# Everything behind attention as one list of steps, ordered for each engine by the kernel itself, with GpSimd's passes moved to VectorE

## The chip, the cores and the metric

One core of a Trainium2 chip. The metric is the device time of one execution in microseconds, as the median of several runs. All inputs and outputs lie in HBM; attention, two gated layers and their projections run in one launch.

## The reference

```python
attn_out = attention(q, k, v, tau)        # q, k, v: (4, 8, 576, 64); scores under max - tau are masked
x = attn_out.transpose(0, 2, 1, 3).reshape(2304, 512)

def moe(x, w_gate, w_val, w_out):         # 512 -> 1536 -> 512
    g = x @ w_gate
    return (g / (1 + exp(-g)) * (x @ w_val)) @ w_out

def moe2(x, w1, w2, w3, w_out):           # 512 -> 1024 -> 1024 -> 512
    return (((x @ w1) * (x @ w2)) @ w3) @ w_out

return moe2(moe(x, ...), ...)
```

The weights come as 64-bit floats (their product with a numpy scalar is one), the rest as 32-bit floats.

## The kernel before

**Number format.** TensorE multiplies in a rounded 32-bit format. Every operand of a large product is held as a pair: a rounded high half and the low half that is left (`high`, `rest`), and each product is three passes (`PASSES`: high x high, high x low, low x high). So for every tile that enters TensorE one engine copies it (ScalarE, the high half) and one subtracts (VectorE or GpSimd, the low half). A 64-bit weight of 128x512 arrives as words and is put together on the way: two mask passes and a combining pass on VectorE (`bits`, `more`), two activations on ScalarE (`conv_power`, L252 and L253), a difference on GpSimd (`conv_less`, L258), a multiply on VectorE (`value`, L1519). A weight "unit" is one such tile; its 512 KB land in a ring of three buffers (`raw`, L227).

**Tiling.** The 2304 tokens are five blocks (512, 512, 256, 512, 512; numbers 0 to 4); blocks 0 and 1 and blocks 3 and 4 form two pairs, block 2 is alone. The hidden width is cut into tiles f of 128. One projection of one block by one f is 12 matmuls of 512 columns (256 for block 2).

**Stages behind attention.**
1. First projections (`plain`): f = 0 to 2 of the gated layer for each block, two projections each. Each block's x is read back from HBM in two halves that GpSimd adds (`x_add`, L1407); TensorE spreads the reciprocal row sums over the partitions (L1422), VectorE multiplies (L1427) and ScalarE and VectorE split (`x_scale`). Beside this `panels` makes sums and differences of x blocks.
2. Gated stage, f = 3 to 11 (`glu_seq`): each pair of blocks takes seven products instead of eight (`seven`, slots p1 to p7 of six matmuls, L1704), with sums of weight blocks and of x panels. Two such chains run slot by slot beside each other, with block 2's two plain projections between (`run`). ScalarE copies intermediate sums out of a chain's bank before the next product adds to that bank (`snap`, L1718); VectorE adds (L1731, L1747, L1762); GpSimd multiplies (L1754, L1764). The result goes to HBM (`h_dram`).
3. Output projection: for each block over f = 0 to 11 four banks collect 12 matmuls per f; h is read back and split (L1942, L1948). x of the second layer is taken out of the banks (`evacuate`) and panels are made again.
4. Bilinear stage, f = 0 to 7: as stage 2 without the activation.
5. The product w3 @ w_out of the second layer (w3 turned on TensorE, L1464), held as "whole" tiles that were converted earlier and parked in HBM (`v_dram`).
6. Last stage: 18 tiles of 128 tokens, 24 matmuls each, then the store.

**What sets the order.** Attention runs by a plan of its own (`Plan`, in a manually scheduled section). Behind it the code issues work in program order, slot by slot, and after each slot calls `feed`/`tick` and `do`, which bring forward one piece of weight conversion and one of the queued pieces (panels, copies). `take` and `give` hand out a common pool of 42 slots of 128x2x512; `spare` and `promised` keep some back. The framework then orders the instructions for each engine with its own model of time. All transfers are issued on SyncE's queue (SP). The same two-chain stages use the banks of PSUM: two double banks S and four single banks T.

Of the kernel before, what the change touches and what calls it, by code (L numbers as in the profile page):

```python
# [28 lines left out]
PLAIN = 3  # L29

# [14 lines left out]
class Plan:  # L45
# [20 lines left out]
    def order(self):  # L66
# [51 lines left out]
        return [step for _, _, step in sorted(done, key=lambda d: d[:2])]  # L118


@with_exitstack
def kernel(
# [1336 lines left out]
    w3v = {}  # L1459

    def w3_turn(i, g, val):
        bank = t_bank()
        for c in range(4):
            nc.tensor.transpose(bank[:, c * P:(c + 1) * P], val[:, c * P:(c + 1) * P], ident)  # L1464
        un = take()
        nc.scalar.copy(out=un[:, 0, :], in_=bank)
        nc.vector.tensor_tensor(
            out=un[:, 1, :], in0=bank, in1=f32(un[:, 0, :]), op=ALU.subtract
        )
        w3v[i, g] = un  # L1470


    units, u_raw = deque(), deque()
    spare, promised = [0], [0]

    def pair_of(srcs, keys, sums=False, want=3):

        shared = {}
        for i, (src, key) in enumerate(zip(srcs, keys)):
            units.append(  # L1480
                {"src": src, "key": key, "i": i, "pair": shared, "sums": sums, "want": want})

    def u_fetch():
        while units and len(u_raw) + len(conv_raw) < N_BIG and units[0].get("raw") is None:
            u = units.popleft()
            u["raw"] = conv_load(u["src"])
            u_raw.append(u)

    def split(un, src, engine):
        nc.scalar.copy(out=un[:, 0, :], in_=src)  # L1490
        engine.tensor_tensor(out=un[:, 1, :], in0=src, in1=f32(un[:, 0, :]), op=ALU.subtract)

    def stages(u):

        pair, key = u["pair"], u["key"]
        if u["i"] == 0:
            pair["stage"] = take(F32)
        m = pair["stage"][:, u["i"], :]
        mi = m.bitcast(I32)
        if wide == 2:  # L1500
            two = u["raw"].rearrange("p (n t) -> p n t", t=2)
            a, x = two[:, :, 0], two[:, :, 1]
            low = u["raw"].bitcast(U16).rearrange("p (n t) -> p n t", t=4)[:, :, 1]

        def bits():
            nc.vector.tensor_scalar(
                out=mi, in0=x, scalar1=(1 << 20) - 1, scalar2=None, op0=ALU.bitwise_and
            )
            nc.vector.tensor_scalar(
                out=x, in0=x, scalar1=-(1 << 20), scalar2=None, op0=ALU.bitwise_and  # L1510
            )

        def more():
            nc.vector.scalar_tensor_tensor(  # L1514
                out=m, in0=low, scalar=2.0 ** -16, in1=mi, op0=ALU.mult, op1=ALU.add
            )

        def value():
            nc.vector.scalar_tensor_tensor(  # L1519
                out=m, in0=m, scalar=2.0 ** 20, in1=f32(a), op0=ALU.add, op1=ALU.mult  # L1520
            )

        def plain_copy():
            nc.vector.tensor_copy(out=m, in_=u["raw"])

        if wide == 2:
            yield bits
            yield more
            yield lambda: conv_power((a, mi, x))
            yield lambda: conv_less((a, mi, x))  # L1530
            yield value
        else:
            yield plain_copy
        if u["want"] == 1:
            if u["i"]:
                yield lambda: nc.sync.dma_start(out=v_dram[key], in_=pair["stage"])
                give(pair.pop("stage"))
            return

        def high(src, name):  # L1540
            def go():
                u[name] = take()
                promised[0] -= 1
                nc.scalar.copy(out=u[name][:, 0, :], in_=src)  # L1544
            return go

        def rest(src, name, key, engine):
            def go():
                un = wu[key] = u[name]
                engine.tensor_tensor(  # L1550
                    out=un[:, 1, :], in0=src, in1=f32(un[:, 0, :]), op=ALU.subtract
                )
            return go

        yield high(m, "un")
        yield rest(m, "un", key, nc.gpsimd)
        if u["sums"] and u["i"]:
            g, v = (pair["stage"][:, i, :] for i in range(2))
            b11, b21, b12, b22 = g[:, 0:2 * P], g[:, 2 * P:], v[:, 0:2 * P], v[:, 2 * P:]

            def less(*args):
                def go():
                    for out, x, y in args:
                        nc.vector.tensor_tensor(out=out, in0=x, in1=y, op=ALU.subtract)
                return go

            yield less((b11, b12, b11), (b12, b22, b12))
            yield less((b22, b22, b11), (b21, b21, b22))
            yield high(g, "c")
            yield rest(g, "c", ("c", key[1]), nc.vector)  # L1570
            yield high(v, "d")
            yield rest(v, "d", ("d", key[1]), nc.vector)
# [372 lines left out]
    def h_low():  # L1945
# [5 lines left out]
        if i:  # L1951
            give(t)
# [278 lines left out]
```

## Time and profile before

| | |
|---|---|
| median of 3 runs | 1149.25 us (1149.05 to 1150.66) |
| the profiled execution's own time | 1149.66 us |
| its span, first to last instruction | 1147.9 us |
| TensorE shown busy | 1073.8 us, 94% |
| VectorE, ScalarE, GpSimd busy | 829.4, 625.1, 609.5 us |
| mean granted clock of TensorE | 0.977 of full |

A busy TensorE in this profile is not one at its peak: its matmuls overlap, and a matmul that starts every 0.23 us is shown as 0.39 long. Time that TensorE loses is found by counting matmuls per stage, not from its busy share. PE is TensorE's matmul, PEld its weight load, DVE VectorE, ACT ScalarE, POOL GpSimd, SPq SyncE's queue of transfers.

### The profile page before, as it was taken

How to read it: one execution, taken by the hardware profiler on the slowest of the kernel's cores; microseconds unless marked ns; L12 is line 12 of the kernel's file. 1: busy time of each engine (PE TensorE's matmuls, PEld its weight loads, DVE VectorE, ACT ScalarE, POOL GpSimd, SP SyncE). 2: the span in 40 equal slices, each digit the busy share in tenths (PEclk: the TensorE clock that was granted, in tenths of full speed). 3: DMA queues.
4: the chain of work that ended last, by engine and by line, in shares of the span. 5: the costliest groups of instructions: out<-in, count | busy, mean ns of one | idle time of the engine just before them, and what ended most of it. 6: DMA issues, size and time to landing. Idle time of an engine off the chain costs nothing. (4 is left out here: it accounts for less than half of the span.)

```text
span 1147.9 us, 17303 instructions
## 1 busy us (share of the span) xinstructions
PE 1073.8 (94%) x5838; PEld 922.4 (80%) x5838; DVE 829.4 (72%) x1432; ACT 625.1 (54%) x1284; POOL 609.5 (53%) x547
## 2 busy tenths in 40 slices
PE   7999999999987999899999798999999899999998
PEld 6989898999666787678788686888788788788887
DVE  7999999999769758888775877933989863444110
ACT  6898989899734355446465445533545433333100
POOL 5898989987546126445565765633554332213100
PEclk9999999999897999999999899999999999999999
DMA  6776776766572114434336755331144423733312
GB/s 170 176 204 173 186 183 168 181 152 167 153 224 94 61 68 160 130 127 163 115 136 207 249 161 186 103 87 42 62 157 159 156 83 134 263 108 102 110 50 52
DMA packets 127208, 162.39 MB, mean 141 GB/s; under 512 B 48688, under 2 KB 83312, under 8 KB 127120
## 3 DMA queue, kind: packets, MB, share of 16 engines
q1 hardware_dynamic: 126976, 161.29, 47.3%
q8 instruction: 46, 0.75, 0.3%
q14 instruction: 42, 0.34, 0.1%
q10 hardware_dynamic: 144, 0.00, 0.0%
HBM read 93.47 MB, written 44.19 MB: 120 GB/s over the span
## 5 line engine op out<-in xcount | busy, mean ns | idle before, releaser
L1438 PE MATMUL t_bank<-slot,slot 128*128 128x512 f32 (+1 forms) x1536 | 316.1, 358 | 0.7 <-ACT slot L1428 0.7
L1438 PEld LDWEIGHTS t_bank<-slot,slot 128*128 128x128 f32 x1536 | 265.4, 190 | 48.7 <-ACT slot L1428 1.1
L1704 PE MATMUL t_bank<-slot,slot 128*128 128x512 f32 x816 | 206.6, 396 | 11.9 <-ACT tmp L1718 11.8
L1704 PEld LDWEIGHTS t_bank<-slot,slot 128*128 128x128 f32 x816 | 152.9, 191 | 45.1 <-ACT tmp L1718 14.0
L1704 PE MATMUL s_bank<-slot,slot 128*128 128x512 f32 x612 | 160.6, 398 | 9.7 <-DVE tmp L1762 4.3
L258 POOL TENSOR_TENSOR raw<-raw 128x512 int32<-128x512 int32 x76 | 91.8, 1212 | 105.2 <-ACT raw L253 80.3
L1704 PEld LDWEIGHTS s_bank<-slot,slot 128*128 128x128 f32 x612 | 113.0, 190 | 35.9 <-DVE tmp L1762 4.9
L202 POOL TENSOR_TENSOR AT<-tmp,AT 128x512 fp32r<-128x512 f32 x102 | 132.2, 1306 | 3.4
L252 ACT ACTIVATE raw<-raw,ebias 128x512 int32<-128x512 int32 x76 | 58.4, 770 | 133.0 <-DVE slot L1514 89.9
L557 ACT ACTIVATE P<-P,stat 128x576 f32<-128x576 f32 x144 | 113.9, 795 | 7.4 <-DVE P L548 7.0
L548 DVE SCALAR_TENSOR_TENSOR P<-E,stat,s_bank 128x576 f32<-128x576 f32 x144 | 114.4, 808 | 1.5
L532 DVE TENSOR_SCALAR_CACHE_REDUCE E<-s_bank 128x576 f32<-128x576 f32 x144 | 107.2, 754 | 8.2 <-PE s_bank L500 7.0
L500 PE MATMUL s_bank<-R,L 128*128 128x288 f32 x512 | 94.8, 308 | 12.6 <-DVE P L548 10.0
L429 PE MATMUL t_bank<-ident,P 128*128 128x128 f32 x640 | 92.5, 278 | 2.8 <-DVE AT L585 1.3
L500 PEld LDWEIGHTS s_bank<-R,L 128*128 128x128 f32 x512 | 73.8, 189 | 20.8 <-DVE P L548 7.1
L1764 POOL TENSOR_TENSOR h<-h,tmp 128x512 f32<-128x512 f32 x34 | 50.6, 1490 | 67.2 <-DVE tmp L1762 59.2
L1550 POOL TENSOR_TENSOR slot<-slot,slot 128x512 fp32r<-128x512 f32 x46 | 65.7, 1431 | 35.0 <-ACT slot L1544 35.0
L429 PEld LDWEIGHTS t_bank<-ident,P 128*128 128x128 f32 x640 | 75.6, 142 | 8.0 <-ACT P L557 2.6
L197 POOL TENSOR_SCALAR AT<-tmp 128x512 fp32r<-128x512 f32 x102 | 64.4, 638 | 30.1 <-ACT tmp L825 28.3
L1544 ACT CAST slot<-slot 128x512 fp32r<-128x512 f32 x80 | 49.1, 618 | 56.9 <-DVE slot L1519 27.0
L1519 DVE SCALAR_TENSOR_TENSOR slot<-slot,raw 128x512 f32<-128x512 f32 x70 | 65.8, 944 | 18.0 <-POOL raw L258 18.0
L893 PE MATMUL t_bank<-AT,sp 128*128 128x288 f32 x448 | 76.9, 304 | 0.5 <-POOL AT L202 0.5
(171 smaller groups left out, 1856.8 us busy)
## 6 DMA issues: line engine op xcount, KB each, us to landing
slot<-h_dram SPq DMA_DIRECT2D x40, 512.0 KB
h_dram<-h SPq DMA_DIRECT2D x34, 512.0 KB
raw<-in_moe_w_dram SPq DMA_DIRECT2D x32, 512.0 KB
raw<-in_moe_w_out_dram SPq DMA_DIRECT2D x20, 512.0 KB
x_dram<-xs SPq DMA_DIRECT2D x64, 144.0 KB
L<-qlo SPq DMA_DIRECT2D x60, 128.0 KB
L<-qhi SPq DMA_DIRECT2D x60, 128.0 KB
raw<-in_moe_w_gate_dram SPq DMA_DIRECT2D x12, 512.0 KB
```

The source lines that it names most:

```text
L202: nc.gpsimd.tensor_tensor(out=lo, in0=src, in1=f32(hi), op=ALU.subtract)
L258: nc.gpsimd.tensor_tensor(out=a, in0=a, in1=x, op=ALU.subtract)
L429: nc.tensor.matmul(bank[:, t * P:(t + 1) * P], lhsT=part, rhs=ident, is_transpose=True, start=(t == 0), stop=(t == len(parts) - 1),)
L500: nc.tensor.matmul(o, lhsT=lhs, rhs=R[:, c:c + HALF], start=(h == hs2[0] and e == 0), stop=(h == hs2[-1] and e == 1),)
L532: nc.vector.tensor_scalar(out=halves(t), in0=sb[:, :, 0:HALF], scalar1=-FAR, scalar2=None, op0=ALU.mult, op1=ALU.min, accum_out=st[:, 0, c],)
L548: nc.vector.scalar_tensor_tensor(out=halves(p_tile(p, i)), in0=halves(t), scalar=st[:, 1, c], in1=sb[:, :, 0:HALF], op0=ALU.is_gt, op1=ALU ...
L557: nc.scalar.activation(out=u, in_=u, func=ACTF.Exp, scale=-FAR, bias=st[:, 0, c], accum_out=sums[p // HP][:, c],)
L893: nc.tensor.matmul(b["t"][:, 0:HALF], lhsT=splits[p, 2][:, 4 * h + c, :, :].rearrange("p a d -> p (a d)"), rhs=AT[h][:, e, c, cs], start=( ...
L1438: nc.tensor.matmul(o, lhsT=lhs(a), rhs=rhs(c), start=(first and i == 0), stop=(last and i == 2))
L1519: nc.vector.scalar_tensor_tensor(out=m, in0=m, scalar=2.0 ** 20, in1=f32(a), op0=ALU.add, op1=ALU.mult)
L1550: engine.tensor_tensor(out=un[:, 1, :], in0=src, in1=f32(un[:, 0, :]), op=ALU.subtract)
L1704: nc.tensor.matmul(bank, lhsT=un[:, a, (off + kk) * P:(off + kk + 1) * P], rhs=xs[kk][:, c, :], start=(start and kk == 0 and i == 0), stop ...
```

## The change

A class `Program` is added. Work behind attention is written as steps with an engine, a length, the time after which the result is seen, the buffers it reads and writes, and a due time; `order` puts them in order for each engine by simulating when each can start, with room in each pool (T, S, tmp, hb, raw, slot), and `run` issues them in that order inside a manually scheduled section. `feed`, `tick`, `do`, `spare` and `promised` are gone. The core:

```diff
+T_X, LEAD = 6.0, 12.0
+class Program:
+    ROOM = {"T": 4, "S": 2, "tmp": N_TMP, "hb": N_HB, "raw": N_BIG}
+    HOP, SLACK, AHEAD = 0.06, 0.15, 3.0
...
+    def pe(cost, emit, reads, writes, after=()):
+        clock[0] += cost
+        return prog.add("PE", cost, cost + 0.2, emit, reads, writes, clock[0] - cost, after)
+    def act(emit, reads, writes, cost=0.48, due=0.0, after=()):
+    def dve(emit, reads, writes, cost=0.6, due=0.0, after=()):
+    def sp(emit, reads, writes, cost=0.6, lands=4.0, due=0.0, after=()):
```

Low halves, exponent differences and multiplies that GpSimd did are VectorE's:

```diff
-        yield rest(m, "un", key, nc.gpsimd)
+        dve(lambda: sub(un["t"][:, 1, :], src(), f32(un["t"][:, 0, :])), [key, (un, 0)],
+            [(un, 1)], 0.6, due + 0.6)
-            yield lambda: conv_less((a, mi, x))
+        dve(lambda: nc.vector.tensor_tensor(out=two(0), in0=two(0), in1=two(1), op=ALU.subtract),
+            both(r), [(r, 0)], 0.6, due + 2 * step)
-                nc.gpsimd.tensor_tensor(out=h, in0=h, in1=k["u3"], op=ALU.mult)
-            nc.gpsimd.tensor_tensor(out=h, in0=h, in1=t, op=ALU.mult)
+        def times(out, a, b, reads, writes):
+            dve(lambda: nc.vector.tensor_tensor(out=out(), in0=a(), in1=b(), op=ALU.mult),
+                reads, writes, 0.6, 2.0)
```

(The exponent difference of the units that attention converts, `conv_less`, stays as it is.) Only the sum of x's halves stays on GpSimd. The scaled x is now kept in the bank, split from there, and for blocks 3 and 4 also copied back by ScalarE:

```diff
+                prog.add("POOL", size(n, 1.4, 0.8), size(n, 1.45, 0.85), lambda t=t, xw=xw: nc.gpsimd.tensor_tensor(
+                    out=xw(), in0=t["t"][:, 0, 0:n], in1=t["t"][:, 1, 0:n], op=ALU.add
...
+                dve(lambda xw=xw, rb=rb: nc.vector.tensor_tensor(
+                    out=rb(), in0=xw(), in1=rb(), op=ALU.mult
...
+                if j != ODD:
+                    act(lambda xw=xw, rb=rb: nc.scalar.copy(out=xw(), in_=rb()), [bk], [wk],
```

The start of the list, and the output projection with blocks 0 and 1 together:

```diff
+    x_block(2, -2.0)
+    unit_pair(raws_left, (("g", 2), ("v", 2)), None, due=2.0, step=0.7)
+    glu_plain(0, 1)
+    x_block(3, 2.0, [prog.add("SP", 0.0, T_X, lambda: None, [], [], -9.0)])
+    glu_plain(1, 1)
+    x_block(4, 2.0, [prog.add("SP", 0.0, T_X, lambda: None, [], [], -9.0)])
+    ready = [prog.steps[-1]]
+    glu_plain(2, 0)
+    glu_plain(2, 1)
+    panels(0, False, ready, 4.0)
+    glu_plain(0, 2)
+    glu_plain(1, 2)
+    weights_f(PLAIN, after=[prog.steps[-1]], due=6.0)
+    glu_plain(2, 2)
+    panels(1, False, ready, 10.0)
+    for j in (3, 4):
+        for f in range(PLAIN):
+            glu_plain(j, f)
...
+    B0 = out_banks(0, True), out_banks(1, False)
+    for f in range(0, NF1, 2):
+        if f + 6 < NF1:
+            out_units(f + 6, after=at_now(), due=2.0, step=1.0)
+        for j in range(2):
+            HS[j, f], HS[j, f + 1] = h_two(h_dram, "h", j, f, -8.0, at_now(LEAD))
+        for e in range(2):
+            for j in range(2):
+                out_slice(j, f + e, B0[j], HS.pop((j, f + e)))
...
+    with tc.manual_schedule():
+        prog.run()
```

In the gated stage the units of f + 1 are converted while f runs, and a pair of whole units beside them for eight of the nine f; in the output projection a tile of h no longer uses the three h buffers but takes slots. What runs inside attention's end is shorter by block 2's loads and sums.

## Rows read from the trace of the kernel before

**Rows 1.** The page's busy line, and the windows table over the slowest stretch of the clock.

```profile
PE 1073.8 (94%) x5838; PEld 922.4 (80%) x5838; DVE 829.4 (72%) x1432; ACT 625.1 (54%) x1284; POOL 609.5 (53%) x547
...
345.50:358.00 12.50, 5.07 (x11) 3.70 (x12) 12.45 (x18) 4.41 (x9) 8.07 (x6) 0.50 0.11 42
```

**Rows 2.** Windows by stage: length, busy PE, PEld, DVE, ACT, POOL, clock, DMA, GB/s.

```profile
321.60:420.30 98.70, 86.15 (x390) 68.56 (x388) 73.05 (x103) 41.03 (x70) 38.07 (x27) 0.93 0.34 113
420.30:638.40 218.10, 201.29 (x962) 166.82 (x960) 167.78 (x241) 118.19 (x209) 119.65 (x90) 0.99 0.46 154
638.40:801.90 163.50, 154.73 (x721) 128.77 (x722) 111.61 (x132) 72.33 (x128) 89.17 (x66) 0.97 0.41 129
801.90:993.80 191.90, 181.35 (x865) 151.31 (x863) 140.57 (x209) 82.64 (x143) 79.31 (x59) 0.98 0.41 136
993.80:1035.30 41.50, 41.45 (x209) 35.47 (x210) 17.79 (x25) 17.73 (x33) 8.38 (x7) 0.96 0.45 147
1035.30:1147.90 112.60, 108.78 (x480) 89.75 (x478) 22.23 (x27) 18.65 (x37) 13.14 (x12) 1.00 0.27 80
```

**Rows 3.** The chain that ended last: start, length, what.

```profile
981.14 4.57 DMA slot<-h_dram
...
988.82 4.90 DMA slot<-v_dram
...
1034.39 0.87 PE t_bank L1464 x8
1035.27 108.83 PE t_bank L1438 x480
```

**Rows 4.** TensorE's timeline in the output projection of block 2: start, length, instructions.

```profile
721.67 1.60 PE L1438 MATMUL s_bank<-slot,slot 128*128 128x256 f32 x12
723.12 1.60 PE L1438 MATMUL s_bank<-h,slot 128*128 128x256 f32 x12
```

**Rows 5.** Groups of matmuls, gated stage (420.3 to 638.4): count, busy, mean ns, idle.

```profile
L1704 PE MATMUL t_bank<-slot,slot 128*128 128x512 f32 x432 | 109.3, 396 | 4.9 <-ACT tmp L1718 4.9
L1704 PE MATMUL s_bank<-slot,slot 128*128 128x512 f32 x312 | 81.0, 395 | 8.6 <-DVE tmp L1762 4.3 <-DVE h L1731 2.4 <-DVE tmp L1747 2.0
L1438 PE MATMUL t_bank<-slot,slot 128*128 128x256 f32 x216 | 31.8, 282 | 0.0
```

**Rows 6.** TensorE's waits behind 290 us: total, times, longest.

```profile
PE t_bank L1704 <- ACT tmp L1718: 11.8, 7, 2.9
PE t_bank L1422 <- DVE tmp L1789: 7.7, 3, 4.9
...
PE t_bank L1464 <- DMA slot<-v_dram: 2.6, 1, 2.6
```

**Rows 7.** Timelines of VectorE and of GpSimd in the first projections.

```profile
346.70 0.68 DVE L1652 TENSOR_TENSOR slot<-slot,slot 128x512 f32<-128x512 f32 x1
347.31 0.68 DVE L1789 TENSOR_TENSOR tmp<-tmp,t_bank 128x512 f32<-128x512 f32 x1
347.90 0.68 DVE L1652 TENSOR_TENSOR slot<-slot,slot 128x512 f32<-128x512 f32 x1
...
349.91 1.75 DVE L244 SCALAR_TENSOR_TENSOR tmp<-raw,tmp 128x512 f32<-128x512 uint16 x1
...
353.38 0.74 DVE L1427 TENSOR_TENSOR slot<-slot,t_bank 128x256 f32<-128x256 f32 x2
...
349.67 1.44 POOL L1407 TENSOR_TENSOR slot<-slot 128x512 f32<-128x512 f32 x1
```

**Rows 8.** Groups of VectorE in the gated stage.

```profile
L1519 DVE SCALAR_TENSOR_TENSOR slot<-slot,raw 128x512 f32<-128x512 f32 x31 | 29.9, 971 | 11.9 <-POOL raw L258 11.9
...
L1506 DVE TENSOR_SCALAR slot<-raw 128x512 int32<-128x512 int32 x32 | 21.8, 703 | 8.7 <-DMA raw<-in_moe_w_out_dram 7.7 <-PE t_bank L1704 0.7 <-PE s_bank L1704 0.2
```

**Rows 9.** The largest group of GpSimd in the gated stage.

```profile
L258 POOL TENSOR_TENSOR raw<-raw 128x512 int32<-128x512 int32 x31 | 37.5, 1212 | 32.2 <-ACT raw L253 23.7 <-DVE slot L1550 5.3 <-DMA raw<-in_moe_w_out_dram 3.2
```

**Rows 10.** What SyncE's queue waited for, behind 320 us.

```profile
SPq L227 <- DVE slot L1519: 212.9, 57, 40.4
```

More of the change, by code (lines that the diff above doesn't have):

```diff
@@ L1794, in run, with step @@
-    def run(seq, each):
-        for one, two, odd in seq:
-            slots = [s for both in zip(one[:5], two[:5]) for s in both]
-            slots += odd + [s for both in zip(one[5:], two[5:]) for s in both]
-            for slot in slots:
-                slot()
-                each()
-    def loose(f, keys):
-        return lambda: give(*(wu.pop((key, f)) for key in keys if (key, f) in wu))
+    def step(j, f):
+        return [lambda: [slot() for slot in plain_slots(j, f)]]
     def early():
@@ new lines, in product, with go @@
+    def product(bank, ap, x, un, off, start, stop, after=()):
+        def go():
+            for kk in range(2):
+                for i, (a, c) in enumerate(PASSES):
+                    nc.tensor.matmul(
+                        ap(), lhsT=un["t"][:, a, (off + kk) * P:(off + kk + 1) * P],
+                        rhs=x[kk]["ap"](c), start=(start and kk == 0 and i == 0),
+                        stop=(kk == 1 and i == 2), skip_group_check=not start,
+                    )
+        return pe(1.365, go, both(un) + x[0]["keys"] + x[1]["keys"], [bank], after)
@@ new lines, in duo, with at_now, x_new @@
+    def duo(one, two, odd):
+        for a, b in zip(one[:5], two[:5]):
+            a()
+            b()
+        for slot in odd:
+            slot()
+        for a, b in zip(one[5:], two[5:]):
+            a()
+            b()
+    def at_now(back=0.0):
+        return [next(
+            s for s in reversed(prog.steps)
+            if s["engine"] == "PE" and s["due"] <= clock[0] - back and s["busy"] > 0.3
+        )]
+    def x_new(j):
+        n = blocks[j][1]
+        xs[j] = [buf("slot") for _ in range(KD * n // 512)]
+        whole[j] = [buf("slot", F32) for _ in range(KD * n // 1024)]
@@ L2140, with whole_back @@
-    run(bil_seq(), each)
-    do_all()
-    give(*xs_slots.pop(ODD))
-    w3_turns(0)
+    for one, two, f in units2:
+        first = at_now()
+        if 1 <= f < NF2 - 1:
+            weights_2(f + 1, after=first, due=4.0, step=1.6)
+        if f >= NF2 - 2:
+            whole_pair(after=first, due=4.0)
+        chains = [seven(pair, g, "12", False, h2_dram, "h2") for pair, g in (one, two)]
+        duo(*chains, plain(ODD, f, "12", False, h2_dram, "h2"))
+    def whole_back(n, due, after):
+        t = buf("slot", F32)
+        sp(lambda: nc.sync.dma_start(out=t["t"], in_=v_dram[n]), [("v", n)], both(t),
+           0.6, 4.0, due - 6, after)
+        return t
```

1130 lines of the change are left out of this document (572 added, 558 removed).

## The prediction

> **What bounds the kernel now.** I read the head of the page first: 1147.9 us of span, TensorE shown busy 94% of it [rows 1]. That 94% is no measure of what is left, since matmuls overlap, so the question is how long TensorE needs when nothing makes it wait. The last stage answers that: 480 matmuls of 512 columns in one unbroken piece of 108.83 us, 0.2267 us each [rows 3]. Twelve of 256 columns start 1.45 us after the twelve before them, 0.1208 us each [rows 4], and eight transposes take 0.87 us [rows 3]. Now the span cut by stages, from the first projection behind attention (321.6 us) on [rows 2], with the matmuls that the loops ask for, and the floor they give:
>
> - first projections, 321.6 to 420.3: 299 wide, 72 narrow, 16 small spreading ones (taken as 12 wide, 4 narrow): 79.7 of 98.7, lost 19.0;
> - gated stage, to 638.4: 746 wide [rows 5] and 216 narrow: 195.2 of 218.1, lost 22.9;
> - output projection, to 801.9: 577 wide, 144 narrow: 148.2 of 163.5, lost 15.3;
> - bilinear stage, to 993.8: 673 wide, 192 narrow: 175.8 of 191.9, lost 16.1;
> - the product of the last two weights, to 1035.3: 39.9 of 41.5, lost 1.6;
> - last stage: 108.8 of 112.6; the 3.8 are its last copy, store and close.
>
> So 74.9 us behind attention are TensorE standing or running slow. The granted clock is 0.93 to 0.99 in the four stages that lose most and 1.00 in the last [rows 2]; from 345.5 to 358, around the three waits for VectorE that come below, it is 0.50, the 1.2 GHz level [rows 1], so part of a stall is paid for twice. The waits name the direct causes [rows 5, 6]: copies of ScalarE out of the bank that the next product adds to, and VectorE's multiplies and adds that free or fill a bank. Those engines are not full on average (VectorE 168 of 218 us in the gated stage, ScalarE 118) [rows 2]; they are late.
>
> Why VectorE is late is seen in its timeline. A two-input pass over 128x512 takes 0.68 us at 346.70 and 347.90, and another such 1.75 us at 349.91 [rows 7]; GpSimd is at work from 349.67 during the long one [rows 7]. In the gated stage the weights' last VectorE pass averages 971 ns, not 680, and waits 11.9 us for GpSimd's difference as well [rows 8]. GpSimd's own pass takes 1212 ns [rows 9].
>
> **What the change does, part by part.** The arithmetic on TensorE is the same, matmul for matmul; attention and its plan stay. So the floor of the span is 1147.9 - 74.9 = 1073.0 us, and the forecast is this floor plus what is still lost.
>
> *GpSimd's passes go to VectorE.* Per f of the gated stage GpSimd gives up ten: four exponent differences, two low halves, four multiplies; at 1212 ns [rows 9] that is 12 us of GpSimd, and ten times 0.60 = 6.0 us of VectorE, because back-to-back passes start 0.59 to 0.61 us apart [rows 7]. Half-width passes and the mask passes start 0.33 to 0.34 us apart (two of them fill 0.74 us [rows 7]). VectorE's whole list for one f is then: a weight unit 2 x 0.34 + 3 x 0.60 = 2.48, with its low half 3.08, twice 6.16; four half-width differences 1.33; two low halves 1.20; two chains of five passes 6.0; the odd block 0.33; and a pair of whole units 4.96. Sum 19.98 us. TensorE needs 84 x 0.2267 + 24 x 0.1208 = 21.94 us for that f. VectorE is 91% full there, below its bound, if the passes run at the undisturbed length; by the same count it is 68% full in the bilinear stage (15.0 of 21.94, no whole units), and 79% in the first two blocks of the output projection (8.6 per 10.9: two units and four low halves). ScalarE gains eight copies of x, 4 us, while it is half idle.
>
> *The order.* Each engine's queue behind attention is now fixed by a list scheduler inside the kernel, whose lengths I compared with the rows: 0.6 for a VectorE pass, 1.365 for six matmuls (1.360 by rows 3), both right. For transfers it assumes 4 to 5 us from issue to landing, and the trace has two on the chain of 4.57 and 4.90 us [rows 3]. So its plan is close to what runs, apart from transfers that queue behind each other.
>
> *First projections.* The stall at 341 to 354 is block 2's scaling: TensorE waits 7.7 us in three pieces for VectorE [rows 6], which sits in long passes beside GpSimd's sums of x. The change puts (0,1), (1,1) and then block 2 in front, and starts blocks 3 and 4 while some 25 us of projections on loaded blocks are there to run (three of 5.44 us and three of 2.90). The twelve remaining sums of x stay on GpSimd (about 14 us by the diff's lengths of 0.8 and 1.4), so VectorE is still lengthened here; TensorE has cover for that. Kept loss between 0 and 19.0; I take 4.
>
> *Gated stage.* Between 0, as in the last stage, and 22.9; 6, nearer 0, because what made VectorE late is gone, but not 0: at 91% a queue forms, and an instruction that waits for a landing holds all behind it. Queued behind such a wait are the adds that free the two double banks, and TensorE waits for those. Waits of this kind exist today: 7.7 us for the weights' transfers in this stage [rows 8].
>
> *Output projection.* Blocks 0 and 1 now run together for each f, so weights are wanted half as fast (a unit per 5.4 us, not 2.7). The price is that all eight banks are held and every h tile lives in a common slot. Between 0 and 15.3; 3.5. *Bilinear stage*: 0 to 16.1; 2, with VectorE at 68%. Among what goes here is its end: the chain runs from 981.14 through two transfers [rows 3], the second issued only at 988.82, and TensorE stands 2.6 us for it [rows 6]; the change issues both while the last chains run. *Last weights' product*: 0.5.
>
> *SyncE.* All transfers stay on its queue. It waited 212.9 us for the raw ring of three [rows 10] with stores behind it; the ring stays three, and now stores and loads stand in planned order. Nothing on TensorE waited for more than the few transfers above, so I cost it at nothing; if a store's wait now holds a load for h, the output projection pays (its bound of 15.3).
>
> Sum: 4 + 6 + 3.5 + 2 + 0.5 = 16; span 1073.0 + 16 = 1089.0. The profiled execution is 1149.66 for 1147.9 of span, the median of the runs is 1149.25, so I add 1.35: **1090 us**, 59 us faster. Attention's own tail (290 to 321.6) is ordered by the framework together with fewer items than before; I leave it at +-2.
>
> **Rivals.** (a) *VectorE is what holds TensorE in the gated stage and at the start.* For it: 91% is planned, and passes beside GpSimd's sums last 1.75. Then the gated stage loses 22.9 as today, the start 13 and the output projection 8: 1073.0 + 44 + 2 + 1.35 = 1120. Against it: nothing but the sums of x is left to lengthen a pass. The Trainium skill, Perfetto Trace Analysis, section "Optimizing Scalar/DVE Operations", speaks for this rival: it advises moving work away from a saturated VectorE, even to GpSimd, though it adds that the two share a read port so that such a move may not help. The change moves the other way, and rows 7 bear out the second half of the sentence; by its first half the time would be rival (a)'s.
>
> (b) *Slower: late transfers in a fixed order.* Some 70 weight units each begin with a VectorE instruction that waits for its landing, with the bank-freeing adds queued behind it. Such waits exist today [rows 8]. If each unit holds TensorE by x us, the loss is 70x; the gain is used up at x = 74.9/70 = 1.07 us. At 1.5 us: 1073.0 + 105 + 1.35 = 1179. For it: the landing is assumed at 5 us where 4.57 and 4.90 were seen with a queue nearly empty. Against it: the transfer engines are at 46% in the gated stage [rows 2], and a late unit is not wanted before the next f.
>
> (c) *The change doesn't do what it says*: VectorE's long passes come from something other than GpSimd, say the transfers, and stay. At 0.9 us a pass the list of one f is 19.98 x 1.5 = 30 us, 8 over TensorE's, eight times: 64 us, which eats the 59: 1154 or, with the starts better covered, no change.
>
> **How the numbers follow.** Forecast (losses of 4 to 30 in all, 1078 to 1104): 0.70. (a), 1104 to 1130: 0.20. (b): 0.06. (c): 0.04. Range 1077 to 1119: it leaves out (b), (c), the upper third of (a), and losses under 3 us. A measurement can tell about 0.2%, 2.3 us. Faster: forecast and (a), 0.90; same: most of (c), 0.03; slower: (b) and the rest of (c), 0.07.
>
> **What would show it.** Right: no GpSimd work behind some 370 us; VectorE passes of 0.68 and 0.42 only; the first product of the gated stage near 405 instead of 420; granted clock 1.00 in nearly all of the stages; no wait of TensorE over 2 us behind 350. Rival (a): the gated stage at 21.9 us per f plus more than 2, with VectorE shown over 95% busy and TensorE waiting for its adds. Rival (b): VectorE idle before the mask passes, released by raw's transfers, and TensorE idle at the same moments. Rival (c): passes over 1 us while GpSimd is silent. I would be wrong altogether if the planned order itself made TensorE stand, for lack of slots or banks, with all engines idle.

## The result, and the profile of the changed kernel

The changed kernel takes **1093.09 us** (median of four runs, 1091.19 to 1095.22), beside 1149.95 us for the kernel before on the same chip: a ratio of 0.9493 between the means, with a 95% interval of 0.9451 to 0.9536. The forecast was 1090 us in a range of 1077 to 1119. The profiled execution took 1094.16 us for a span of 1092.3 us, and the rows below are from it.

First the busy line of the page and its row of the granted clock (40 slices of the span, in tenths), which answer [rows 1]:

```profile
PE 1053.9 (96%) x5838; PEld 912.6 (84%) x5838; DVE 849.1 (78%) x1679; ACT 635.6 (58%) x1292; POOL 275.3 (25%) x300
...
PEclk9999999999989999999999899999999999999999
```

Then the span behind attention by stages, which answers [rows 2]. The columns are the same: the stretch, its length, busy time of PE, PEld, DVE, ACT and POOL with their instructions, granted clock, share of the DMA engines, GB/s.

```profile
323.90:406.50 82.60, 79.50 (x379) 64.04 (x377) 60.96 (x104) 39.50 (x71) 14.14 (x12) 1.00 0.42 138
406.50:604.50 198.00, 197.84 (x974) 167.75 (x973) 188.08 (x346) 126.19 (x210) 0.00 (x0) 1.00 0.51 172
604.50:762.20 157.70, 151.83 (x721) 126.87 (x720) 116.00 (x211) 77.88 (x138) 0.00 (x0) 0.98 0.47 161
762.20:938.90 176.70, 176.00 (x866) 148.96 (x865) 135.84 (x236) 76.52 (x131) 0.00 (x0) 1.00 0.29 105
938.90:979.70 40.80, 40.44 (x210) 33.89 (x209) 18.37 (x31) 15.01 (x29) 0.00 (x0) 1.00 0.55 194
979.70:1092.30 112.60, 108.86 (x481) 89.82 (x479) 27.28 (x46) 23.07 (x45) 0.00 (x0) 1.00 0.31 89
```

GpSimd is silent from the gated stage on. VectorE is busy 188 of 198 us there, 95%, and yet TensorE loses next to nothing: 974 matmuls need 197.9 us by the prediction's unit times. (These are the 962 of the prediction and 12 more: in the kernel before, 12 matmuls of the gated products filled gaps among the first projections, and now they run in their own stage. So that both stages hold as many matmuls as here, the kernel before is cut 12 matmuls earlier than in [rows 2], at 417.8, and the two stages are then 96.2 and 220.6 us long. The tables below use that cut.)

TensorE's waits behind 290 us, which answer [rows 6] (total us, times, longest):

```profile
PE t_bank L1605 <- DVE slot L1692: 5.0, 3, 3.6
PE t_bank L596 <- DVE AT L752: 2.9, 2, 1.7
...
PE t_bank L1852 <- ACT tmp L1871: 0.7, 1, 0.7
...
PE s_bank L1852 <- DVE tmp L1882: 0.2, 1, 0.2
```

The 11.8 us for ScalarE's copies (4.9 of them in the gated stage [rows 5], the rest in the bilinear one) are 0.7 us, all in the bilinear stage, and the 7.7 us for VectorE's scaling of block 2 are gone. What is left, beside waits of up to 1.0 us, is one of 3.6 us at the start of the output projection, and the end of attention (L596).

VectorE's groups between 410 and 600 us, which answer [rows 8] (busy us, mean ns of one, idle time before them):

```profile
L1746 DVE TENSOR_TENSOR raw<-raw 128x512 int32<-128x512 int32 x36 | 24.7, 687 | 2.7 <-ACT raw L420 2.5
L1748 DVE SCALAR_TENSOR_TENSOR slot<-slot,raw 128x512 f32<-128x512 f32 x36 | 24.7, 686 | 0.4
...
L1734 DVE TENSOR_SCALAR slot<-raw 128x512 int32<-128x512 int32 x35 | 14.7, 420 | 0.0
L1692 DVE TENSOR_TENSOR slot<-slot 128x256 f32<-128x256 f32 x32 | 13.6, 424 | 0.8
```

The weights' last pass (L1748) averages 686 ns where it took 971 [rows 8], the mask pass 420 where it took 703, and neither the 11.9 us of waiting for GpSimd nor the 7.7 us for a transfer is left. The difference of L1746, which GpSimd made in 1212 ns [rows 9], is a VectorE pass of 687 ns.

### The profile page after: what moved, and what is told of

It reads as the page before. It is cut to its first block, busy times and chain, and to the rows that moved or that the text cites. A ratio compares the mean times of both kernels' runs of the same rounds, so it can differ in the third digit from the quotient of the medians.

```text
span 1092.3 us, 17043 instructions
## 1 busy us (share of the span) xinstructions
PE 1053.9 (96%) x5838; PEld 912.6 (84%) x5838; DVE 849.1 (78%) x1679; ACT 635.6 (58%) x1292; POOL 275.3 (25%) x300
## 4 chain that ended last, share of the span: by engine, by line
PE 56%; DVE 8%; ACT 1%; issue 1%; DMA 1%; SPq 0%; ACTq 0%; DVEq 0%
PE t_bank L1605 23%; PE t_bank L1852 16%; PE s_bank L1852 11%; PE s_bank L1605 6%; DVE slot L1692 3%; DVE slot L1829 1%; DMA slot<-v_dram 1%; DVE raw L1746 1%; DVE slot L1742 1%; DVE slot L1748 1%; PE t_bank L2241 1%; DVE h L1878 0%; DVE tmp L1882 0%; DVE raw L1737 0%; DVE slot L1734 0%
## 5 line engine op out<-in xcount | busy, mean ns | idle before, releaser
L1605 PE MATMUL t_bank<-slot,slot 128*128 128x512 f32 (+1 forms) x1680 | 340.4, 361 | 7.4 <-DVE slot L1692 5.0
L1605 PEld LDWEIGHTS t_bank<-slot,slot 128*128 128x128 f32 x1680 | 284.4, 189 | 58.8 <-DVE slot L1692 6.4
L1852 PE MATMUL t_bank<-slot,slot 128*128 128x512 f32 x816 | 196.8, 390 | 0.7 <-ACT tmp L1871 0.7
L1852 PEld LDWEIGHTS t_bank<-slot,slot 128*128 128x128 f32 x816 | 151.9, 188 | 32.2 <-ACT tmp L1871 1.4
L1692 DVE TENSOR_TENSOR slot<-slot,slot 128x512 fp32r<-128x512 f32 (+1 forms) x238 | 147.6, 658 | 35.9 <-ACT slot L2124 24.7
L1852 PE MATMUL s_bank<-slot,slot 128*128 128x512 f32 x612 | 147.3, 389 | 0.2 <-DVE tmp L1882 0.2
L1852 PEld LDWEIGHTS s_bank<-slot,slot 128*128 128x128 f32 x612 | 114.8, 188 | 24.4 <-DVE tmp L1882 0.6
L1871 ACT COPY tmp<-t_bank 128x512 f32<-128x512 f32 x102 | 59.4, 583 | 113.4 <-PE t_bank L1852 113.2
L1700 ACT CAST slot<-slot 128x512 fp32r<-128x512 f32 x134 | 80.6, 621 | 57.0 <-DVE slot L1692 24.6
L596 PE MATMUL t_bank<-ident,P 128*128 128x128 f32 x640 | 93.1, 280 | 4.9 <-DVE AT L752 2.9
L1605 PE MATMUL s_bank<-slot,slot 128*128 128x512 f32 (+1 forms) x432 | 86.5, 359 | 0.9 <-DVE tmp L1882 0.9
L596 PEld LDWEIGHTS t_bank<-ident,P 128*128 128x128 f32 x640 | 76.5, 144 | 10.0 <-ACT P L724 2.7
L1605 PEld LDWEIGHTS s_bank<-slot,slot 128*128 128x128 f32 x432 | 72.7, 192 | 13.3 <-DVE tmp L1882 1.6
```

Of the source, the lines that this page charges most:

```text
L596: nc.tensor.matmul(bank[:, t * P:(t + 1) * P], lhsT=part, rhs=ident, is_transpose=True, start=(t == 0), stop=(t == len(parts) - 1),)
L1605: nc.tensor.matmul(o, lhsT=lhs(a), rhs=rhs(c), start=(first and i == 0), stop=(last and i == 2))
L1700: act(lambda: nc.scalar.copy(out=un["t"][:, 0, :], in_=src()), [key], [(un, 0)], 0.52, due, after)
L1852: nc.tensor.matmul(ap(), lhsT=un["t"][:, a, (off + kk) * P:(off + kk + 1) * P], rhs=x[kk]["ap"](c), start=(start and kk == 0 and i == 0), ...
```

## The experiments

Two theories stood against each other at first. *Shared reads*: GpSimd's passes make VectorE's long while they run, so moving them is what gains. *Order*: the list scheduler gains, and the moved passes only fit into it. Stage lengths in us, from the windows of each run:

| | before | passes moved, old order | new order, passes on GpSimd | changed kernel | units later |
|---|---|---|---|---|---|
| up to the first projection behind attention | 321.6 | 320.9 | 324.6 | 323.9 | 325.6 |
| first projections | 96.2 | 98.0 | 92.1 | 82.6 | 82.6 |
| gated stage | 220.6 | 198.2 | 218.2 | 198.0 | 197.5 |
| output projection | 163.5 | 153.0 | 178.2 | 157.7 | 149.9 |
| bilinear stage | 191.9 | 178.7 | 181.3 | 176.7 | 176.3 |
| last weights' product | 41.5 | 42.3 | 40.3 | 40.8 | 40.9 |
| last stage | 112.6 | 112.6 | 112.6 | 112.6 | 112.6 |

**Only the move.** The kernel before with its own order; GpSimd's passes behind attention become VectorE's, all but the sums of x's halves. The core:

```diff
-            yield lambda: conv_less((a, mi, x))
+            yield lambda: nc.vector.tensor_tensor(out=a, in0=a, in1=x, op=ALU.subtract)
...
-        yield rest(m, "un", key, nc.gpsimd)
+        yield rest(m, "un", key, nc.vector)
...
-            nc.gpsimd.tensor_tensor(out=h, in0=h, in1=t, op=ALU.mult)
+            nc.vector.tensor_tensor(out=h, in0=h, in1=t, op=ALU.mult)
```

> The kernel before, in the framework's order, with every GpSimd pass behind attention except the sums of x's halves given to VectorE; nothing else. Theory 'shared reads' (VectorE is late because its passes are lengthened while GpSimd reads; the order is the rest): VectorE's two-input passes in the gated stage fall from 0.9 to 0.97 us to about 0.69, the stage loses 8 to 14 us instead of 22.9, total 1115 to 1135. Rival 'order alone' (where a pass runs does not matter): passes shorter, but the stage loses as before, total 1140 to 1160.

Measured: 1106.21 us, 0.9601 of before (0.9568 to 0.9633). That is better than both theories allowed: some 44 us come from this alone. By windows of the gated stage, and TensorE's waits from 320 to 420 us, of this kernel:

```profile
418.90:617.10 198.20, 198.20 (x974) 167.67 (x973) 175.94 (x332) 123.05 (x211) 0.00 (x0) 1.00 0.50 169
```

```profile
PE t_bank L1422 <- DVE tmp L1789: 7.6, 4, 4.4
PE t_bank L1422 <- DMA tmp<-r_dram: 2.6, 1, 2.6
```

The gated stage has no loss left, in the old order. The move takes two things away at once, the lengthening of VectorE's passes and VectorE's waits for GpSimd's results, which in the kernel before come to 21.3 us in that stage:

```profile
DVE slot L1519 <- POOL raw L258: 13.5, 12, 1.9
...
DVE slot L1564 <- POOL slot L1550: 4.2, 3, 2.4
DVE tmp L1747 <- POOL raw L258: 3.6, 1, 3.6
```

VectorE is busier than before (175.9 us of 198.2, against 168.5 of 220.6), so it was not for want of its time that TensorE stood. How much of the 44 us belongs to the lengthening and how much to the waits, no run here separates; the runs with extra passes below show the lengthening alone, on a VectorE that is nearly full.

The first projections keep their loss: TensorE waits 7.6 us, as before (7.7 [rows 6]), nearly all of it for the scaling of block 2. GpSimd, VectorE and TensorE there:

```profile
337.27 10.24 POOL L1407 TENSOR_TENSOR slot<-slot 128x512 f32<-128x512 f32 x6 [0.46 <-DMA slot<-x_dram]
...
344.64 1.74 DVE L1662 TENSOR_TENSOR slot<-slot,slot 128x512 fp32r<-128x512 f32 x1
...
349.51 0.68 DVE L1662 TENSOR_TENSOR slot<-slot,slot 128x512 fp32r<-128x512 f32 x1
...
349.05 0.58 PE L1422 MATMUL t_bank<-tmp,pick 8*128 8x256 f32 x1 [4.42 <-DVE tmp L1789]
352.38 0.58 PE L1422 MATMUL t_bank<-tmp,pick 8*128 8x256 f32 x1 [2.76 <-DVE tmp L1789]
```

The prediction's reading was that VectorE "sits in long passes beside GpSimd's sums". Much of the wait of 4.42 us agrees: the sums run until 347.51, and VectorE's passes are long until then. The wait of 2.76 us does not: GpSimd is silent and the passes take 0.68 us, but several others stand in the queue before block 2's. So both causes are seen here, and the changed list removes both, as the next run shows.

**Only the order.** The changed kernel, in whose list the passes go back to GpSimd with a length of 1.05 to 1.25 us each. The list is put in order again for these lengths, and x of blocks 2 to 4 is still read out of the banks:

```diff
-        dve(lambda: nc.vector.tensor_tensor(out=two(0), in0=two(0), in1=two(1), op=ALU.subtract),
-            both(r), [(r, 0)], 0.6, due + 2 * step)
+        pool(lambda: psub(two(0), two(0), two(1)), both(r), [(r, 0)], 1.05, due + 2 * step)
...
-            dve(lambda: nc.vector.tensor_tensor(out=out(), in0=a(), in1=b(), op=ALU.mult),
-                reads, writes, 0.6, 2.0)
+                pool(lambda: nc.gpsimd.tensor_tensor(out=out(), in0=a(), in1=b(), op=ALU.mult),
+                     reads, writes, 1.25, 2.0)
```

> The changed kernel with GpSimd's passes given back where the kernel before had them (exponent differences, low halves of the units, chain multiplies, every second panel and h low half), in a list that knows their lengths (1.05 and 1.25 us); the steps and due times are the same. By the list's own lengths VectorE has 146 us less. Theory 'shared reads': VectorE's two-input passes average over 0.85 us in the gated stage and TensorE loses 8 to 20 us there instead of 0.4; total 1105 to 1130. Rival 'order alone': within 5 us of 1093.

Measured: 1149.57 us, 0.9974 of before (0.9948 to 0.9999). Both theories missed: the order alone gains nothing that counts. It isn't idle, though: it takes 4 us off the first projections, 2 off the gated stage and 11 off the bilinear stage, and gives 15 back in the output projection and 3 at attention's end. Block 2's scaling no longer stops TensorE, although the sums run here as well. VectorE's groups from 422 to 630 us, in its gated stage, show why little is won there:

```profile
L1757 DVE SCALAR_TENSOR_TENSOR slot<-slot,raw 128x512 f32<-128x512 f32 x36 | 38.6, 1072 | 29.1 <-POOL raw L1689 29.1
...
L1898 DVE TENSOR_TENSOR tmp<-s_bank,tmp 128x512 f32<-128x512 f32 x33 | 22.6, 686 | 9.5 <-ACT tmp L1883 8.4 <-PE s_bank L1864 0.3
```

Of the stage's 218.2 us VectorE is busy 177.0, and of the 41.2 in which it is idle it stands 38.6 in front of these two groups, 29.1 for GpSimd's difference. The plan counted a VectorE pass as 0.6 us, the spacing of passes that are shown as 0.68; here the full-width groups with two inputs from SBUF average 0.88 to 1.12, and those with one input from a bank stay at 0.69. GpSimd's passes take 1.10 to 1.48 where the plan has 1.05 and 1.25. Whether a list made from these lengths would have gained, no run here shows.

**Extra GpSimd passes beside.** In the changed kernel, 80 additions of two 128x512 inputs are put on GpSimd in the gated stage, two at each of the 40 places where a tile is split into its halves or a whole unit stored; their results go to a slot that nobody reads.

```diff
+    beside, extra = [False], buf("slot", F32)
+
+    def by_pool(un, key, ap, due):
+        for n in range(2 if beside[0] else 0):
+            prog.add("POOL", 1.25, 1.3, lambda: nc.gpsimd.tensor_tensor(
+                out=extra["t"][:, 0, :], in0=ap(), in1=ap(), op=ALU.add),
+                [(un, key)], [(extra, 0)], clock[0] + due + 1.3 * n)
...
+        by_pool(un, 0, lambda: f32(un["t"][:, 0, :]), due + 0.6)
```

> The changed kernel with 80 additional GpSimd passes of 128x512 in the gated stage, each reading two inputs from SBUF into a slot nobody reads (two behind each weight tile and each whole tile); VectorE's, ScalarE's and TensorE's steps are unchanged in number. Theory 'shared reads': VectorE's passes beside them last up to 1.8 us, and as VectorE is 95% busy in that stage (188 of 198 us) the stage grows by 30 to 80 us; total 1120 to 1170. Rival 'order alone', or passes lengthened by transfers: within 5 us of 1093, passes stay at 0.68.

Measured: 1141.99 us in one run; the gated stage grows from 198.0 to 247.9 us. That undoes 49 of the 57 us of gain with work that nothing waits for. VectorE's timeline around 453 us, and GpSimd's, in which four additions run as one piece from 452.64 to 458.02:

```profile
452.56 0.68 DVE L1892 TENSOR_TENSOR tmp<-s_bank,tmp 128x512 f32<-128x512 f32 x1
453.16 1.07 DVE L1751 SCALAR_TENSOR_TENSOR slot<-raw,slot 128x512 f32<-128x512 uint16 x1
454.15 0.68 DVE L1892 TENSOR_TENSOR tmp<-s_bank,tmp 128x512 f32<-128x512 f32 x1
454.75 2.37 DVE L1692 TENSOR_TENSOR slot<-slot,slot 128x512 fp32r<-128x512 f32 x2
457.05 1.52 DVE L1755 TENSOR_TENSOR raw<-raw 128x512 int32<-128x512 int32 x1
```

```profile
452.64 5.38 POOL L1701 TENSOR_TENSOR slot<-slot 128x512 f32<-128x512 f32 x4 [3.06 <-ACT slot L1708]
```

Under one and the same GpSimd piece, a pass (454.15) that reads a bank and SBUF takes 0.68 us, and those that read SBUF twice take 0.92 to 1.5. So GpSimd being busy does not lengthen every pass; what the pass reads matters.

**Which GpSimd work does it.** The same 80 places, once with a pass that writes a constant and reads nothing, once with a plain copy of one input (the results again unread). The edits are shown against the run with additions.

```diff
-            prog.add("POOL", 1.25, 1.3, lambda: nc.gpsimd.tensor_tensor(
-                out=extra["t"][:, 0, :], in0=ap(), in1=ap(), op=ALU.add),
+            prog.add("POOL", 1.25, 1.3, lambda: nc.gpsimd.memset(extra["t"][:, 0, :], 0.0),
```

> The changed kernel with 80 extra GpSimd passes over 128 x 512 in the gated stage, at the places of the extra additions that cost 48 us, but these only write (a constant, to a slot that nobody reads) and read nothing. If reads of SBUF by GpSimd lengthen VectorE's passes: the time stays within 5 us of 1093, VectorE's two-input passes in the gated stage stay at 0.68 to 0.70 us. If any GpSimd work on SBUF beside lengthens them: 1115 to 1145 us, two-input passes near 1 us.

```diff
-            prog.add("POOL", 1.25, 1.3, lambda: nc.gpsimd.tensor_tensor(
-                out=extra["t"][:, 0, :], in0=ap(), in1=ap(), op=ALU.add),
+            prog.add("POOL", 1.25, 1.3, lambda: nc.gpsimd.tensor_copy(
+                out=extra["t"][:, 0, :], in_=ap()),
```

> The changed kernel with the 80 extra GpSimd passes as plain copies (one input of 128 x 512 from SBUF, written to a slot that nobody reads). If one reading stream of GpSimd is enough to hold VectorE's two-input passes: 1110 to 1145 us, those passes at 0.9 us or more. If two inputs on both engines are needed: within 5 us of 1093, passes at 0.68 to 0.70.

Measured: 1099.52 us with the writes and 1111.56 us with the copies. By the two profiled spans the writes cost 5.5 us, 1097.8 against 1092.3. Of these 5.4 lie ahead of the first projection (it starts at 329.3 instead of 323.9), where there are no extra passes yet; the gated stage is 199.9 us, 1.9 longer, and 1.8 come back behind it. So the total missed its bound of 5 us by a stretch that the edit doesn't touch, and the stage says what was asked. VectorE's groups from 410 to 600 us, beside the writes and then beside the copies:

```profile
L1754 DVE TENSOR_TENSOR raw<-raw 128x512 int32<-128x512 int32 x35 | 24.0, 687 | 1.8 <-ACT raw L420 1.8
...
L1745 DVE TENSOR_SCALAR raw<-raw 128x512 int32<-128x512 int32 x35 | 17.3, 495 | 1.2
L1742 DVE TENSOR_SCALAR slot<-raw 128x512 int32<-128x512 int32 x35 | 16.8, 481 | 0.0
```

```profile
L1755 DVE TENSOR_TENSOR raw<-raw 128x512 int32<-128x512 int32 x32 | 28.1, 878 | 0.3 <-ACT raw L420 0.3
...
L1892 DVE TENSOR_TENSOR tmp<-s_bank,tmp 128x512 f32<-128x512 f32 x31 | 21.1, 682 | 0.0
L1746 DVE TENSOR_SCALAR raw<-raw 128x512 int32<-128x512 int32 x31 | 13.3, 430 | 1.1
```

These are means over passes that ran beside a GpSimd pass and passes that didn't. In the gated stage of the run with copies 15 of 37 passes of L1755 ran beside one and took 1.09 to 1.10 us; the other 22 took 0.69. Beside writes that doesn't happen: 30 two-input passes lay nine tenths or more under them and took 0.67 to 0.69. First a stretch beside ten writes, then one beside six copies:

```profile
438.19 0.67 DVE L1750 SCALAR_TENSOR_TENSOR slot<-raw,slot 128x512 f32<-128x512 uint16 x1
...
439.63 0.72 DVE L1745 TENSOR_SCALAR raw<-raw 128x512 int32<-128x512 int32 x1
...
435.54 6.61 POOL L1701 MEMSET slot<- 128x512 f32 x10
```

```profile
448.08 0.68 DVE L1751 SCALAR_TENSOR_TENSOR slot<-raw,slot 128x512 f32<-128x512 uint16 x1
...
450.90 1.10 DVE L1755 TENSOR_TENSOR raw<-raw 128x512 int32<-128x512 int32 x1
...
447.56 5.94 POOL L1701 COPY slot<-slot 128x512 f32<-128x512 f32 x6 [3.04 <-ACT slot L1708]
```

So writes leave the two-input passes alone, and a copy, one stream of reads, lengthens most of them, but not all: L1751, one of whose inputs is 16-bit, stays at 0.68 beside copies, and the copies themselves last from 0.62 to 1.14 us. The Trainium skill, SBUF — State Buffer, section "Who interferes with whom", states this rule: a VectorE instruction with two SBUF inputs contends with a GpSimd one that reads SBUF, and not with one that only writes. These three runs agree with both halves, apart from L1751 beside the copies. The mask passes, with one input, do grow beside writes: the eight of L1745 that lay nine tenths or more under them took 0.71 to 0.72 us where they take 0.43 alone. What copies or the extra additions would do to them these runs don't show, because no mask pass ran beside one. In the kernel before, where they ran beside GpSimd's two-input passes, some took up to 1.5.

**How full VectorE may be.** A fifth of the extra additions, 16 (against the run with 80):

```diff
-        for n in range(2 if beside[0] else 0):
+        calls[0] += beside[0]
+        for n in range(2 if beside[0] and calls[0] % 5 == 1 else 0):
```

> The changed kernel with 16 instead of 80 extra GpSimd additions of two inputs in the gated stage (their results go to a slot that nobody reads). With 80 VectorE's passes there grew by some 53 us in sum, 0.66 us for each, and the stage by 50. If what counts is VectorE's queue against TensorE's time: 16 lengthen VectorE's 188 us by 10.5, to 198.6 of the stage's 198, so the stage stays at 198 to 202 us and the run within 5 us of 1093. If every GpSimd pass beside costs the stage by itself (0.6 us each, as the 80 did): 207 to 209 us for the stage, 1102 to 1105 us in all.

Measured: 1100.71 us, the gated stage 205.6 us, between the two: the slack that I had counted, all of the 10 us that VectorE is idle, isn't there. Put side by side, the gated stages of these runs, one profile each:

| extra GpSimd passes | VectorE busy, us | stage, us | share |
|---|---|---|---|
| none (changed kernel) | 188.1 | 198.0 | 95.0% |
| 80 writes | 193.1 | 199.9 | 96.6% |
| 16 additions | 199.5 | 205.6 | 97.0% |
| 80 copies | 209.4 | 215.4 | 97.2% |
| 80 additions | 242.3 | 247.9 | 97.7% |

In the four runs with extra passes VectorE is idle for 5.6 to 6.8 us, whatever the length of the stage: there it sets the stage, and every microsecond more on it is about one more of time. Without them it is idle for 9.9, and TensorE's 198 us stand. 198 - 6 = 192, so by these rows the changed kernel is some 4 us of VectorE's time, half a microsecond for each f, away from the point at which VectorE sets the stage. All of these runs load VectorE through GpSimd; none gives it more passes of its own.

**Two pairs of output weights ahead.** The one long wait of the changed kernel is at the start of the output projection. TensorE's and VectorE's timelines there:

```profile
604.48 0.39 PE L1605 MATMUL t_bank<-slot,slot 128*128 128x512 f32 x1
608.43 3.80 PE L1605 MATMUL t_bank<-slot,slot 128*128 128x512 f32 x11 [3.57 <-DVE slot L1692]
613.10 1.22 PE L1605 MATMUL s_bank<-slot,slot 128*128 128x512 f32 x2 [0.87 <-DVE tmp L1882]
```

```profile
604.55 0.69 DVE L1746 TENSOR_TENSOR raw<-raw 128x512 int32<-128x512 int32 x1 [1.62 <-ACT raw L420]
605.28 0.69 DVE L1748 SCALAR_TENSOR_TENSOR slot<-slot,raw 128x512 f32<-128x512 f32 x1
605.89 2.49 DVE L1692 TENSOR_TENSOR slot<-slot,slot 128x512 fp32r<-128x512 f32 x4
```

The low halves that TensorE needs (L1692) stand in VectorE's queue behind the end of a weight unit, which itself waited 1.62 us for ScalarE. And ScalarE, ahead of that unit's activations, had waited for two tiles of h to land:

```profile
600.31 0.62 ACT L2124 CAST slot<-slot 128x512 fp32r<-128x512 f32 x1 [1.48 <-DMA slot<-h_dram]
...
602.45 0.62 ACT L2124 CAST slot<-slot 128x512 fp32r<-128x512 f32 x1 [0.99 <-DMA slot<-h_dram]
```

The edit converts the third pair of output weights two steps later, not ahead of the stage:

```diff
-    for f in range(0, 6, 2):
+    for f in range(0, 4, 2):
         out_units(f, after=gate, due=-16.0 + f, step=1.0)
...
-        if f + 6 < NF1:
-            out_units(f + 6, after=at_now(), due=2.0, step=1.0)
+        if f + 4 < NF1:
+            out_units(f + 4, after=at_now(), due=-2.0, step=1.0)
```

> The changed kernel with two pairs of output-projection weight units converted ahead of that stage instead of three; the later ones follow two f later each, 4 us earlier relative to TensorE. Theory 'VectorE's queue' (the 3.6 us stall at 604.5 and the half clock behind it come from six weight units standing in front of the first h tiles' low halves): the stall goes, TensorE's clock stays full there, 5 to 8 us faster, 1085 to 1088. Rival 'late transfers' (ScalarE waited 1.5 and 1.0 us for the first h tiles to land): under 2 us gained.

Measured: **1085.79 us** (1085.39 to 1087.21), 0.9418 of before (0.9393 to 0.9443), faster than both kernels. The output projection takes 149.9 us in place of 157.7, at a granted clock of 1.00 instead of 0.98, and TensorE's waits for L1692 from 600 to 757 us are down to two, 1.5 us in all. The edit takes the pair's passes out of VectorE's queue and its loads out of SyncE's at once; in this run ScalarE waits for no landing there. Which of the two was worth how much isn't separated.

**Left-over units later.** On top of that, the conversion of the two weight units that attention leaves over goes behind the first projection of block 0:

```diff
-    unit_pair(raws_left, (("g", 2), ("v", 2)), None, due=2.0, step=0.7)
     glu_plain(0, 1)
+    unit_pair(raws_left, (("g", 2), ("v", 2)), None, after=at_now(), due=6.0, step=0.7)
```

> The changed kernel with the output weights' third pair converted later (as in the run at 1085.8 us), and with the two units left over by attention converted behind the start of the second set of gated products instead of at once. If these conversions in VectorE's queue are what ends attention 2.3 us later than before: the first projection behind attention starts at 321.0 to 322.5 us instead of 323.9, and the time is 1083 to 1085 us. If something else ends attention later: the first projection stays at 323.5 or later and the time at 1085 to 1087.

Measured: 1087.04 us (1085.69 to 1091.35). The first projection starts at 321.8 us as the theory wanted, 2.1 us sooner than in the changed kernel. Starts of single profiles vary more than that (323.9 to 329.3 in the runs that keep the conversions in place), but most of that lies ahead of 300 us, where the edit touches nothing. From the start of an earlier group of attention's matmuls (L816, at 299.44 us in the changed kernel and 299.20 here) to the first projection it is 24.2 to 25.7 us in all eight profiles with the conversions in place, 22.6 here, and 22.6 in the kernel before. So those conversions are what delays attention's end. But the total didn't follow: the first projections take 85.1 us, not 82.6, since TensorE now waits for VectorE in them:

```profile
PE s_bank L2029 <- DVE slot L1692: 2.2, 2, 2.0
```

The passes only changed the place at which they are in the way.

**An order made for faster transfers.** The list is put in order as if transfers landed after 0.4 of their assumed time, so each queue asks for data earlier than it comes:

```diff
-            step["start"], step["seen"] = t, t + step["until"]
+            step["start"], step["seen"] = t, t + step["until"] * (0.4 if step["engine"] == "SP" else 1.0)
```

> The changed kernel, whose order is made as if every transfer landed after 0.4 of the time that the plan otherwise assumes; on the chip the transfers stay as they are, so the fixed order asks for their data earlier than they come. If late transfers in a fixed order decide (the prediction's rival, from 1.07 us more per unit), the waits of TensorE for transfers and converted units grow and the time goes above 1110 us. If the buffers loaded ahead cover that, the time stays within 8 us of the changed kernel's 1093, with no wait of TensorE over 3 us for a transfer in the gated stage.

Measured: 1101.09 us (1097.10 to 1105.36), 8.0 above the changed kernel, on the bound between the two. The gated stage of the profiled run (the 1097.10) is 198.2 us with no wait of TensorE for a transfer, and its longest wait behind 290 us is 2.8; 3.0 us are lost in the bilinear stage, 1.4 at attention's end. By the spans of the two profiles it is 2.9 us above the changed kernel, and the intervals of the two ratios to the kernel before (0.9529 to 0.9620 here) overlap. So a plan this wrong about transfers costs at most some 8 us; rival (b) would have been 86 above the changed kernel. Only the fastest of its four runs has a trace.

## Why the prediction was right, point by point

**The floor** stood: 1073.0 us of span, and what is kept above it measures 19.3, forecast 16. That these two are so close is in part luck: the gated stage kept 6 us less than forecast and the output projection 6 more. By terms (stage length less the matmuls' time; 12 matmuls, 2.7 us, count for the gated stage and not for the first projections):

| term | forecast | measured | working |
|---|---|---|---|
| first projections | 4 | 5.6 | 82.6 - 77.0 |
| gated stage | 6 | 0.1 | 198.0 - 197.9 |
| output projection | 3.5 | 9.5 | 157.7 - 148.2 |
| bilinear stage | 2 | 0.9 | 176.7 - 175.8 |
| last weights' product | 0.5 | 0.9 | 40.8 - 39.9 |
| attention's end | 0, +-2 | 2.3 | 323.9 - 321.6 |

**The output projection is the mis-sized term.** 3.57 and 0.87 us of it are the two waits shown above. Behind the first, and around the second, the clock is at the 1.2 GHz level:

```profile
609.90:616.80 6.90, 6.03 (x15) 4.22 (x15) 6.87 (x14) 2.74 (x5) 0.00 (x0) 0.51 0.68 269
```

The matmuls in it take 6.0 us at 0.51 of the clock, so 3.0 us are lost; with the waits that is 7.4, and the run with two pairs ahead gains 157.7 - 149.9 = 7.8. The prediction named weights being wanted half as fast as the effect of the joined blocks, and the banks they hold as its price. It didn't ask what the gated stage's end must carry: three pairs of units, two blocks of h and the last chains, all on a VectorE that is 95% full. And it put SyncE's queue at nothing, with the output projection to pay if a load for h comes late; ScalarE's 1.48 and 0.99 us in front of the stall are waits for such loads.

**The gated stage** was forecast to lose 6 us to a queue on VectorE; it lost 0.1. The reason for putting it near 0 (passes of 0.68 and 0.42 only) is in the groups shown above, and the runs with extra passes show what longer ones cost. VectorE's count was 91% and the profile has 95%: the prediction's list has 34 weight units at most (two for each f and eight pairs), and 36 to 38 ran, because output weights are converted ahead here. That is close to rival (a)'s premise, without its consequence. By the table of shares its price of 22.9 us would take some 27 us more of VectorE's time (198 + 22.9 - 6 = 215).

**What the prediction joined and the runs take apart** is the move and the order. It gave the move as what makes VectorE punctual, and the order as what mends the first projections. The move alone is worth 44 of the 56 us of span; the order with the move another 11 (first projections 15 less, output projection 5 more, attention's end 3 more, bilinear stage and last product 4 less); the order without the move 0.6. What the move gains through shorter passes and what through fewer waits for GpSimd stays open. The cause named for the stall at 341 to 354 us, VectorE's long passes beside GpSimd's sums, is half of it: with the move alone the sums still run, and 2.76 of the 7.6 us fall where they don't. Nor did the sums lengthen VectorE's passes in the changed kernel, as the prediction expected: the full-width ones stay at 0.69 to 0.70 us while the sums run behind 349 us, and each reads one of its inputs from a bank.

**Attention's end** came 2.3 us later, just past the +-2. The conversions of the left-over units are put among its last passes: moved away, the stretch behind 299 us, in which 1.9 of the 2.3 us lie, is as short as in the kernel before.

**The rivals.** (a), 1120: VectorE does not hold TensorE in the gated stage. The sentence of the Trainium skill that spoke for it (Perfetto Trace Analysis, "Optimizing Scalar/DVE Operations") says that a saturated VectorE may be relieved even by GpSimd. Here it is the reverse: 80 copies on GpSimd, which take nothing from VectorE but read beside it, add 21.3 us to VectorE's busy time. Its second half, that the two share a read port and such a move might not help, fits. (b), late transfers, 1179: TensorE waits directly for no transfer behind attention, and not in the run whose order counts on faster ones either. A late landing is seen only through ScalarE, in front of the one long stall. (c), long passes that have another cause, 1154: passes over 0.7 us are gone from the gated stage with GpSimd, and come back with its reads.

**Signs named ahead.** GpSimd's last pass ends at 362 us (370 said), the first gated product starts at 406.6 (405 said), the clock is 1.00 in five of six stages. "No wait of TensorE over 2 us behind 350" failed, by the one of 3.57.

## What to carry to other kernels

Where two-input passes on VectorE come out longer than their usual time, look for GpSimd reading SBUF under them; such a pass may be cheaper on VectorE itself, even at 95% of its time. Test an order and a change of engines apart: here the order was worth nothing while GpSimd kept its passes, and 11 us once they were moved. And a stage that VectorE fills to 95% has no room for the next stage's work: see what stands in its queue where the stages meet.

## What was not expected of the hardware

- VectorE can be 95% busy without TensorE losing 0.2 us to it, and the limit was sharp: at 96.6% the stage was 1.9 us longer, and from 97.0 to 97.7% its length was VectorE's busy time and some 6 us (205.6, 215.4 and 247.9 us).
- GpSimd's two-input additions slow down as well: the sums of x over 128x512 average 1290 ns in the changed kernel, where VectorE reads a bank beside them, and 1751 in the run with the move alone, where VectorE reads SBUF twice.
- One-input mask passes on 32-bit integers, at 420 ns (430 for the second of them), grow beside GpSimd's writes: the second takes 711 to 716 where it lies under them. Two-input passes don't.
- After a stall of 3.57 us, with one more of 0.87 within, TensorE was at the 1.2 GHz level for 6.9 us: 3.0 us lost to the clock beside 4.4 of waiting.
